# Decayed k tiles used in place as score operands, with every fourth row given to the fourth head pair

## The chip, the cores and the metric

One NeuronCore of one Trainium2 chip runs the whole program. The metric is the device time of one execution in microseconds (us). Kernels are compared by the median of their runs.

## The reference

The inputs are four batches of eight heads, 768 steps, 48 dimensions per head (float32). Three layers follow each other. The change touches the first alone, a linear attention whose state decays by a gate of its own in every dimension of the key:

```
f = sigmoid(f_logit)
for t in range(768):
    state = f[:, :, t, :, None] * state + einsum('bhd,bhe->bhde', k[:, :, t], v[:, :, t])
    y[:, :, t] = einsum('bhd,bhde->bhe', q[:, :, t], state)

x     = y, heads side by side: (4, 768, 384)
theta = x @ w_theta                                   # layer 2
u     = x + w_tok_r @ (x * cos(theta)) + w_tok_i @ (x * sin(theta))
x     = u + relu(u @ w_ch)
h     = relu(x @ w_in)                                # layer 3
out   = (h[:, :, :512] * (w_spatial @ norm(h[:, :, 512:]) + b_spatial)) @ w_out
```

## The kernel before, in words

**Stages.** The program has a prologue (attention of batch 0), then a long mixed stage in which layer 2 of batch b runs among the attention of batch b + 1, and from about 370 us a last stage with layer 3 alone. The change touches nothing of the last stage.

**Chunks and decay.** The 768 steps are cut into 12 chunks of 64. `dense(b, g)` (L494) takes 128 of the 384 rows (head, dimension) of a batch at a time, so that no partition is empty: three dense tiles a batch, twelve in all. It loads f, k and q, makes the running products of the gates inside a chunk (a scan on DVE into `icp`, a logarithm and an exponential on ACT into `cw`) and multiplies k by `icp` and q by `cw`. GpSimd writes the chunks' decay into 12 more columns of the k tile.

**Pairs.** Everything after that goes by pairs of heads, four a batch, 16 in all, numbered u. TensorE works there on quadrants of 64 x 64. A head has only 48 rows, so a pair needs tiles with head 0 in partitions 0 to 47, head 1 in 64 to 111, and zeros between: `KP` (768 + 12 columns) and `QP` (768 columns), two buffers of each, whose zeros are written once. `att_load` (L541) fills them with DMAs from the dense tiles, by runs of at most 48 partitions, split where a head crosses from one dense tile into the next; it loads v in two layouts (`VN`, `VC`) as well.

**Per pair.** `att_s` (L585) makes the scores k^T q of each chunk (tile psc), which DVE masks into `sc`. `att_w` (L557) multiplies the transposed k, tile `KT`, which `att_k` (L530) makes from the dense tile with six transposes (tile pt), by v (tile pw); ACT copies the products out, ACT also spreads the decay over a tile (cu in batch 0, later st or cb), and a DVE scan turns both into the states. For pairs up to `NEAR` the states are read as the scan leaves them, 12 elements apart; for later ones ACT copies them to adjacent elements first (tile st). `att_x` (L603) adds q times state and score times v (tile px), and ACT copies the pair's columns into `X`. Layer 2 of a batch starts with transposes of `X` (tile pt) and can start only when all four pairs are in it. Its large product over the steps has the name acc, the product by w_ch the name hh; tk is a token weight, z a product of x and a sine or cosine, both made on DVE and ACT; ws is a landing tile for weights.

**What sets the order.** Within a stage the program is issued by ticks written by hand (`UNIT`, `KEYS`, `DECAY`, L52 to L58, in `mixes`); a planner (`Plan`) then reorders each engine's list with its own table of durations. Each engine runs its list in that order. All DMAs are issued by one queue, SyncE's, in its own planned order: an issue that has to wait for a tile holds up all behind it. Nearly all instructions are recorded at one helper line, L370 (L371 in the changed kernel), so tiles are told apart by name.

**Buffers.** Dense tiles take turns in `BUFS` buffers (f 1, k 2, q 2); the few in `EARLY` borrow the space of tiles that layer 2 needs later.

Of the kernel before, what the change touches and what calls it, by code (L numbers as in the profile page):

```python
# [21 lines left out]
P = 128  # L22
B, H, S, D = 4, 8, 768, 48
DM = H * D
# [13 lines left out]
PARTS = 4  # L38
BUFS = {"f": 1, "k": 2, "q": 2}

EARLY = {("f", 1): "z10", ("f", 2): "z11", ("k", 2): "z12", ("q", 2): "z13"}

# [7 lines left out]

NEAR = 8
WARM = {("s", 0, 0): 20}  # L52
# [19 lines left out]
class Box:  # L72
    def __init__(self, ap):
        a = ap.bass_ap
        self.t = a.tensor.name
        shape, dims = list(a.tensor.shape), [list(x) for x in a.ap]
        row = math.prod(shape[1:])
        span = lambda d: sum(abs(s) * (n - 1) for s, n in d) + 1
        if dims[0][0] == row and len(dims) > 1:
            self.p = (a.offset // row, a.offset // row + dims[0][1])  # L80
# [310 lines left out]
class Kernel:  # L391
# [75 lines left out]
    def att_open(self, ctx):  # L467
        tc, V, A, G = self.tc, self.V, self.A, self.G
        self.a1 = a1 = self.pool(ctx, "a1", 1, side="left")
        self.a2 = self.pool(ctx, "a2", 2, side="left")  # L470
        self.mask = a1.tile([P, C], F32, name="mask")
        G.memset(self.mask, 1.0)
        for h in range(2):
            m = self.mask[64 * h : 64 * h + 64, :]
            G.affine_select(out=m, in_=m, pattern=[[1, C]], compare_op=ALU.is_ge, fill=0.0, base=0, channel_multiplier=-1)
        self.one = a1.tile([P, NC, C], BF16, name="one")
        G.memset(self.one, 0.0)
        G.memset(self.one[:, :, 0:1], 1.0)
# [4 lines left out]
        self.KP = [a1.tile([P, S + NC], F32, name=f"kp{i}") for i in range(2)]  # L483
        self.QP = [a1.tile([P, S], F32, name=f"qp{i}") for i in range(2)]
        self.SC = [a1.tile([P, S], F32, name=f"sc{i}") for i in range(2)]
        self.KT = a1.tile([P, NT, DM + 64 - D], F32, name="kt")
        for i in range(2):
            G.memset(self.KP[i], 0.0)
            G.memset(self.QP[i], 0.0)
        G.memset(self.KT[:, :, DM:], 0.0)  # L490
        self.dn, self.un = {}, {}


    def dense(self, b, g):  # L494
# [4 lines left out]
        for x in ("f", "k", "q"):  # L499
# [3 lines left out]
            else:  # L503
                t[x] = self.a2.tile([P, w], F32, name=f"{x}{n}", tag=x, bufs=BUFS[x])
            self.Q.dma_start(out=t[x][:, 0:S], in_=self.a[x].rearrange("u r t -> (u r) t")[P * n : P * n + P])
        f, k, q, cx = t["f"][:, 0:S], t["k"][:, 0:S], t["q"][:, 0:S], t["k"][:, S:]
# [23 lines left out]
    def att_k(self, b, g):  # L530
        self.group()
        k = self.dn[3 * b + g]["k"]
        for n in range(0, NT, 3):
            p = self.bank("pt")
            self.warm(p, ("k", b, g, n))
            for i in range(3):
                self.T.transpose(p[:, P * i : P * i + P], k[:, P * (n + i) : P * (n + i) + P], self.ident)
            self.A.activation(self.KT[:, n : n + 3, P * g : P * g + P], p[:, 0:DM].rearrange("p (n d) -> p n d", n=3), AF.Copy)


    def att_load(self, u):  # L541
        b, pr, w = u // NP, u % NP, u % 2
        for x, to in (("k", self.KP[w]), ("q", self.QP[w])):
            for h in range(2):
                r, end = D * (2 * pr + h), D * (2 * pr + h + 1)
                o = 64 * h
                while r < end:
                    m = min(end, r // P * P + P) - r
                    self.Q.dma_start(out=to[o : o + m], in_=self.dn[3 * b + r // P][x][r % P : r % P + m])
                    r, o = r + m, o + m  # L550
        self.Q.dma_start(out=self.VN[w], in_=self.a["vu"][u])
        self.Q.dma_start(out=self.VC[w], in_=self.a["va"][u])
# [4 lines left out]
    def att_w(self, u):  # L557
        self.group()
        V, A, T = self.V, self.A, self.T
        w2 = u % 2  # L560
        KT, VN = self.KT, self.VN[w2]
        if u < NP:
            cu = self.c1.tile([P, 2, D, NC], F32, name=f"cu{u}", tag=f"uT{w2}")
            cb, ub = cu[:, 0], cu[:, 1]
        else:
            far = u >= NEAR
            cb, ub = [self.a2.tile([P, D, NC], F32, name=f"{n}{u}", tag=n, bufs=m) for n, m in (("cb" if far else "st", 2 - far), ("ub", 1))]
        A.activation(cb, self.KP[w2][:, None, S:].to_broadcast([P, D, NC]), AF.Copy)
        w = [self.bank("pw") for _ in range(2)]
        self.warm(w[0], ("w", u))  # L570
        w = [x[:, 0 : 6 * D].rearrange("p (n d) -> p n d", n=NT) for x in w]
        for n in range(NT):
            for s, i in ((0, 0), (1, 1), (1, 0), (0, 1)):
                o, r, h = slice(64 * i, 64 * i + 64), slice(64 * s, 64 * s + 64), 2 * (u % NP) + i
                T.matmul(w[s][o, n], lhsT=KT[r, n, D * h : D * h + 64], rhs=VN[r, i, n], start=True, stop=True)
        for s in range(2):
# [8 lines left out]
    def att_s(self, u, g):  # L585
        self.group()
        V, T = self.V, self.T
        K, Q, sc = self.KP[u % 2], self.QP[u % 2], self.SC[u % 2]
        ps = self.bank("psc", "acc" if u < NP else "att")
# [13 lines left out]
    def att_x(self, u, X):  # L603
        self.group()
        A, T, pr = self.A, self.T, u % NP
        Q, sc, v, st = self.QP[u % 2], self.SC[u % 2], self.VC[u % 2], self.st[u]
        ps = [self.bank("px") for _ in range(2)]
# [521 lines left out]
    def mixes(self, X, sa, sw, se):  # L1129
# [35 lines left out]
        for u in range(NP, B * NP):  # L1165
# [4 lines left out]
            at(t + 2, self.att_s, u, 1)  # L1170
            at(t + XLAG, self.att_x, u, x)
        for g, t in enumerate(DECAY):
            steps(self.dense((g + 4) // 3, (g + 4) % 3), [t + k for k in range(3)])
        for b in range(1, B):
            steps(self.p1_thetas(b, X[b % 2]), [2 * n * (b - 1) + n + t for t in THETA[b - 1]])
# [26 lines left out]
    def run(self):  # L1202
# [26 lines left out]
        for _ in range(FILL):  # L1229
            self.T.matmul(p[:, 0:P], lhsT=self.ident, rhs=self.ident, start=True, stop=True)  # L1230
        self.att_k(0, 0)
        run(merge((dense(0, 1), 9), (self.att_pe(0, X[0]), 6)))
        self.att_k(0, 1)
        run(merge((dense(0, 2), 9), (self.att_pe(1, X[0]), 6)))
        self.att_k(0, 2)
        run(pe(2))
# [58 lines left out]
def layout(inputs):  # L1295
# [5 lines left out]
    def heads(x):  # L1301
        return c(x.transpose(0, 1, 3, 2).reshape(B * NP, 2 * D, S))

    raw = lambda x: x.view(np.uint64) if x.dtype == np.float64 else x
    v = inputs["v"]
# [3 lines left out]
    return {  # L1309
        "q": heads(inputs["q"]),  # L1310
        "k": heads(inputs["k"]),
        "f": heads(inputs["f_logit"]),
        "vt": c(v2.transpose(0, 1, 2, 4, 3).reshape(B * NP, 2, D, S)),
# [24 lines left out]
```

## Time and profile before

| | us |
|---|---|
| runs: 618.46, 618.77, 624.06; median | 618.77 |
| the profiled execution, whole | 619.71 |
| the profiled execution, span of the trace | 617.9 |
| TensorE matmuls busy (5736 instructions) | 589.9 (95%) |
| DVE busy (822) | 457.7 (74%) |
| ACT busy (622) | 332.0 (54%) |
| GpSimd busy (54) | 21.3 (3%) |
| moved by DMA | 146.57 MB, 237 GB/s |

The execution's own time holds 1.8 us around the span. An engine's share over the whole span is a mean over stages with different limits; where TensorE stood idle or was clocked down, and what released it, says more. A busy TensorE is not one at its peak: matmuls overlap, and their ends are modelled.

### The profile page before, as it was taken

Reading aid. Unit: us, or ns where it says so; the run is one execution under the profiler, and the core shown is the slowest. Engines: PE = TensorE matmul, PEld = TensorE weight load, DVE = VectorE, ACT = ScalarE, POOL = GpSimd, SP = SyncE. Lnnn points to the kernel's source line nnn. Section 1 sums busy time; section 2 is a strip of 40 time slices with the busy share of each in tenths; the row PEclk is TensorE's granted clock in tenths of the full one; section 3 lists DMA queues with packets and bytes.
Section 4 is the critical chain, followed back from the end, with each engine's and each line's share of the span. In section 5 each row is a group of like instructions: output and inputs, shape, how many; then the busy total and the mean of one; then the engine's idle time right before and its main releaser. Section 6 shows DMA issues by size and latency. Waiting matters only on the chain.

```text
span 617.9 us, 14127 instructions
## 1 busy us (share of the span) xinstructions
PE 589.9 (95%) x5736; PEld 534.2 (86%) x5736; DVE 457.7 (74%) x822; ACT 332.0 (54%) x622; POOL 21.3 (3%) x54
## 2 busy tenths in 40 slices
PE   8678999999999999989999999999999999999995
PEld 8566556766899899979999988999999999999995
DVE  5776999887799668827998538897659656966681
ACT  4555783558867587736884224533453345345421
POOL 4200010000010000000000000000000000000000
PEclk9967999999999999999999999999999999999998
DMA  7788958989778978888999989598109712950322
GB/s 278 225 259 244 298 191 238 284 289 321 245 215 262 334 267 274 266 271 270 331 307 327 350 284 317 206 339 306 46 15 379 258 39 75 357 192 16 131 101 81
DMA packets 67720, 146.57 MB, mean 237 GB/s; under 512 B 6848, under 2 KB 35264, under 8 KB 67648
## 3 DMA queue, kind: packets, MB, share of 16 engines
q1 hardware_dynamic: 67648, 145.59, 70.4%
q8 instruction: 47, 0.77, 0.5%
q14 instruction: 25, 0.20, 0.1%
HBM read 104.20 MB, written 31.85 MB: 220 GB/s over the span
## 4 chain that ended last, share of the span: by engine, by line
PE 83%; DVE 6%; DMA 5%; issue 2%; ACT 2%; POOL 0%; SPq 0%; DVEq 0%; ACTq 0%
PE acc L370 21%; PE pg L370 14%; PE pu L370 8%; PE pv L370 8%; PE po L370 8%; PE hh L370 6%; PE pth L370 6%; PE px L370 4%; PE psc L370 4%; PE pt L370 3%; DMA kp<-k 2%; PE pw L370 2%; DVE tk L370 2%; DVE icp L370 1%; DMA wpd<-wt 1%
## 5 line engine op out<-in xcount | busy, mean ns | idle before, releaser
L370 PE MATMUL acc<-tk,z 128*128 128x384 f32 x792 | 174.3, 369 | 1.8 <-DVE tk L370 1.2
L370 PEld LDWEIGHTS acc<-tk,z 128*128 128x128 f32 x792 | 137.7, 188 | 18.7 <-DVE tk L370 1.8
L370 PE MATMUL pg<-sp,vn 128*128 128x384 f32 x504 | 88.0, 336 | 0.0
L370 PEld LDWEIGHTS pg<-sp,vn 128*128 128x128 f32 x504 | 87.4, 188 | 0.0
L370 PE MATMUL po<-wo,gt 128*128 128x384 f32 x288 | 52.3, 339 | 0.0
L370 PEld LDWEIGHTS po<-wo,gt 128*128 128x128 f32 x288 | 50.8, 188 | 0.8 <-ACT gt L370 0.5
L370 PE MATMUL pu<-x,wi 128*128 128x384 f32 x288 | 50.7, 334 | 0.0
L370 PEld LDWEIGHTS pu<-x,wi 128*128 128x128 f32 x288 | 50.1, 188 | 0.3
L370 PE MATMUL pv<-wi,x 128*128 128x512 f32 x216 | 50.4, 390 | 0.0
L370 PEld LDWEIGHTS pv<-wi,x 128*128 128x128 f32 x216 | 40.5, 188 | 8.1
L370 PE MATMUL hh<-uT,wc 128*128 128x384 f32 x216 | 42.7, 344 | 1.3 <-DVE xt L370 0.9
L370 PEld LDWEIGHTS hh<-uT,wc 128*128 128x128 f32 x216 | 37.8, 188 | 3.0 <-DVE uT L370 1.3
L370 DVE TENSOR_TENSOR vn<-vr,vn 128x768 fp32r<-128x768 f32 x24 | 22.9, 956 | 19.6 <-ACT vn L370 18.8
L370 ACT ACTIVATE gt<-g 128x384 fp32r<-128x384 f32 x32 | 16.7, 523 | 38.0 <-DVE g L370 38.0
L370 DVE BATCH_NORM_STATS2 st<-vr 128x6 f32<-128x512 f32 x24 | 16.5, 691 | 25.7 <-ACT vr L370 25.6
L370 PE MATMUL psc<-qp,kp 64*64 64x64 f32 x768 | 30.0, 226 | 4.4 <-DMA kp<-k 3.1
L370 PEld LDWEIGHTS psc<-qp,kp 64*64 64x64 f32 x768 | 26.9, 140 | 8.2 <-issue 2.9
L370 PE MATMUL px<-vc,sc 64*64 64x48 f32 x768 | 29.7, 230 | 3.3 <-issue 3.3
L370 ACT ACTIVATE vn<-vr 128x768 fp32r<-128x768 f32 x24 | 20.3, 845 | 21.9 <-PE pg L370 18.8
L370 ACT ACTIVATE ws<-ws 128x768 f32<-128x768 f32 (+2 forms) x28 | 20.6, 740 | 19.5 <-DMA ws<-wo_dram 8.2
L370 PEld LDWEIGHTS px<-vc,sc 64*64 64x64 f32 x768 | 27.3, 150 | 3.8 <-issue 3.6
L370 PE MATMUL pth<-ft,xt 128*128 128x384 f32 x72 | 25.5, 493 | 0.6 <-ACT xt L370 0.6
(128 smaller groups left out, 1002.0 us busy)
## 6 DMA issues: line engine op xcount, KB each, us to landing
sp<-wpd SPq DMA_DIRECT2D x56, 576.0 KB, 6.2
tk<-tkp SPq DMA_DIRECT2D x48, 384.0 KB, 4.9
ws<-tok_dram SPq DMA_DIRECT2D x12, 768.0 KB, 5.7
tkp<-tk SPq DMA_DIRECT2D x24, 384.0 KB, 4.5
f<-f_dram SPq DMA_DIRECT2D x12, 384.0 KB, 5.8
k<-k_dram SPq DMA_DIRECT2D x12, 384.0 KB, 6.0
q<-q_dram SPq DMA_DIRECT2D x12, 384.0 KB, 6.7
vn<-vu_dram SPq DMA_DIRECT2D x16, 288.0 KB, 6.1
```

The source lines that it names most:

```text
L370: r = f(*a, **k)
```

## The change

The rows of q, k and f are put into another order on the way in (`layout`, function `dense`). Each dense tile of 128 rows now holds two heads in two groups of 64 partitions; in each group three rows out of four belong to that head (48 rows), and every fourth (16 rows) belongs to one of the heads 6 and 7. Three dense tiles hold heads 0 to 5 and, in their fourth rows, all 96 rows of heads 6 and 7.

So for three pairs of four the k tile is used where it lies: its foreign rows are made harmless by zeros in q. `att_mask` copies q to `QP` on ACT with a factor per partition, `live`, that is 0 in every fourth row and 1 elsewhere (GpSimd and DVE make it once). The fourth pair alone is gathered by DMA: `att_gap` copies every fourth partition, 32 rows of k and of q from each dense tile (as 16 + 16 from the middle one, where heads 6 and 7 meet), into the one `KP` and the third `QP`. For that pair the columns of `KT` that `att_w` loads as weights stand 4 elements apart.

The k tiles live longer, so they have three buffers and q has one; one more q tile is in `EARLY`; one tick of `DECAY` moves from 51 to 58, and `NEAR` from 8 to 6, so that pairs 6 and 7 also get the copy to adjacent states.

```diff
-BUFS = {"f": 1, "k": 2, "q": 2}
-EARLY = {("f", 1): "z10", ("f", 2): "z11", ("k", 2): "z12", ("q", 2): "z13"}
+BUFS = {"f": 1, "k": 3, "q": 1}
+STEP, GAP = 4, C - D
+EARLY = {("f", 1): "z10", ("f", 2): "z11", ("k", 2): "z12", ("q", 1): "z14", ("q", 2): "z13"}
...
-NEAR = 8
+NEAR = 6
...
-DECAY = [0, 4, 19.5, 36, 40, 45, 51, 73]
+DECAY = [0, 4, 19.5, 36, 40, 45, 58, 73]
...
+        m = a1.tile([P, P // STEP], F32, name="rows")
+        G.memset(m, 1.0)
+        G.affine_select(out=m, in_=m, pattern=[[-STEP, P // STEP]], compare_op=ALU.not_equal, fill=0.0, base=1 - STEP, channel_multiplier=1)
+        V.tensor_reduce(self.live, m, axis=AX.X, op=ALU.min)
...
+    def att_gap(self, b, g):
+        n = 2 * GAP
+        for x, to in (("k", self.KP), ("q", self.QP[2])):
+            gap = self.dn[3 * b + g][x][STEP - 1 : P : STEP]
+            r = n * g
+            while r < n * g + n:
+                i = r // D
+                m = min(n * g + n, D * i + D) - r
+                self.Q.dma_start(out=to[C * i + r % D : C * i + r % D + m], in_=gap[r - n * g : r - n * g + m])
+                r += m
+
+    def att_kq(self, u):
+        b, pr = u // NP, u % NP
+        return (self.dn[3 * b + pr]["k"], self.QP[u % 2]) if pr < 3 else (self.KP, self.QP[2])
+
+    def att_mask(self, u):
+        self.A.activation(self.QP[u % 2], self.dn[3 * (u // NP) + u % NP]["q"], AF.Copy, scale=self.live[:, 0:1])
 
     def att_load(self, u):
-        b, pr, w = u // NP, u % NP, u % 2
-        for x, to in (("k", self.KP[w]), ("q", self.QP[w])):
-            for h in range(2):
-                r, end = D * (2 * pr + h), D * (2 * pr + h + 1)
-                o = 64 * h
-                while r < end:
-                    m = min(end, r // P * P + P) - r
-                    self.Q.dma_start(out=to[o : o + m], in_=self.dn[3 * b + r // P][x][r % P : r % P + m])
-                    r, o = r + m, o + m
+        w = u % 2
         self.Q.dma_start(out=self.VN[w], in_=self.a["vu"][u])
...
-        A.activation(cb, self.KP[w2][:, None, S:].to_broadcast([P, D, NC]), AF.Copy)
+        A.activation(cb, K[:, None, S:].to_broadcast([P, D, NC]), AF.Copy)
...
-                T.matmul(w[s][o, n], lhsT=KT[r, n, D * h : D * h + 64], rhs=VN[r, i, n], start=True, stop=True)
+                if u % NP < 3:
+                    o2, step = DM * n + P * (u % NP) + C * i, 1
+                else:
+                    o2, step = DM * n + STEP * D * i + STEP - 1, STEP
+                k = KT[r, o2 : o2 + (C - 1) * step + 1 : step]
+                T.matmul(w[s][o, n], lhsT=k, rhs=VN[r, i, n], start=True, stop=True)
...
+        def after(n, t):
+            b, g = n // 3, n % 3
+            u = NP * b + g
+            x, y = max(t, done(NP * b - 1)), max(t, done(u - (NP if g == 1 else 2)))
+            at(x, self.att_gap, b, g)
+            at(y, self.att_mask, u)
+            return max(x, y)
```

**Where the order moves.** The first place is ACT's list in the prologue, from the first transposed k on. In it f, q, k are dense tiles (one number each per tile), cu is the state tile of a pair, kp and qp the padded operands. Before:

```order
L370 ACTIVATE kt<-pt 128x3x128 x2
L370 ACTIVATE cw<-icp 128x768
L370 ACTIVATE cw<-cw 128x768
L370 ACTIVATE f_381<-f_381 128x768 x2
L370 ACTIVATE cu_276<-kp_104 128x576
L370 ACTIVATE cu_276<-pw 128x288 x2
L370 ACTIVATE cw<-icp 128x768
L370 ACTIVATE X_129<-px 128x6x48 x2
```

And now:

```order
L371 ACTIVATE kt<-pt 128x3x128 x2
L371 ACTIVATE cu_278<-k_137 128x576
L371 ACTIVATE cu_278<-pw 128x288 x2
L371 ACTIVATE cw<-icp 128x768
L371 ACTIVATE cw<-cw 128x768
L371 ACTIVATE qp_105<-q_139,live 128x768
L371 ACTIVATE f_388<-f_388 128x768 x2
L371 ACTIVATE qp_106<-q_225,live 128x768
L371 ACTIVATE cu_425<-k_223 128x576
```

The masked copies of q for pairs 0 and 1 are new on ACT, and the decay of a pair is read from the k tile itself.

The second place is SyncE's queue at the same time, from the load of the third k tile on. Before:

```order
L370 DMA k_383<-k_dram 128x768
L370 DMA kp_104<-k_134 48x780 x2
L370 DMA qp_106<-q_136 48x768 x2
L370 DMA kp_105<-k_134 32x780
L370 DMA qp_107<-q_136 32x768
L370 DMA vc_103<-va_dram 128x576
L370 DMA q_385<-q_dram 128x768
L370 DMA qp_107<-q_219 48x768
L370 DMA kp_105<-k_217 48x780
L370 DMA qp_107<-q_219 16x768
```

And now:

```order
L371 DMA kp<-k_137 32x780
L371 DMA qp_107<-q_139 32x768
L371 DMA vn_100<-vu_dram 128x576
L371 DMA ws<-wt_dram 128x768 x2
L371 DMA f_755<-fd_dram 128x768
L371 DMA kp<-k_223 16x780 x2
L371 DMA qp_107<-q_225 16x768 x2
L371 DMA k_757<-kd_dram 128x768
L371 DMA q_759<-qd_dram 128x768
L371 DMA vc_102<-va_dram 128x576
```

What is gathered there now is for the fourth pair only, and loads of weights and of the next batch stand earlier among the gathers.

The third place is ACT's list later in the prologue, round the transposes of the third k tile; ws is a weight that has landed. Before:

```order
L370 ACTIVATE f_761<-f_761 128x768
L370 ACTIVATE kt<-pt 128x3x128 x2
L370 ACTIVATE cu_602<-kp_105 128x576
L370 ACTIVATE cu_557<-pw 128x288 x2
L370 ACTIVATE cw<-icp 128x768
L370 ACTIVATE ws<-ws 128x384
```

And now:

```order
L371 ACTIVATE X_132<-px 128x6x48 x2
L371 ACTIVATE ws<-ws 128x384
L371 ACTIVATE cw<-icp 128x768
L371 ACTIVATE ws<-ws 128x384
L371 ACTIVATE kt<-pt 128x3x128 x2
L371 ACTIVATE cw<-cw 128x768
L371 ACTIVATE cu_551<-pw 128x288 x2
```

The copies of the transposes (kt) stood ahead of the weights' first step; now two such steps stand ahead of them.

## Rows read from the trace of the kernel before

**Rows 1.** Stretches of 10 us: each engine's busy time (instructions), TensorE's granted clock, DMA share, GB/s.

```profile
20.00:30.00 10.00, 5.51 (x194) 4.86 (x194) 7.81 (x10) 4.34 (x9) 1.13 (x2) 1.00 0.72 207
30.00:40.00 10.00, 7.00 (x170) 6.43 (x172) 7.40 (x12) 5.56 (x11) 0.88 (x2) 0.56 0.74 221
50.00:60.00 10.00, 9.13 (x120) 6.85 (x113) 5.81 (x12) 6.42 (x15) 0.25 (x2) 0.75 0.86 262
80.00:90.00 10.00, 9.86 (x92) 6.04 (x94) 9.73 (x13) 8.50 (x12) 0.98 (x1) 1.00 0.82 273
160.00:170.00 10.00, 10.00 (x138) 9.13 (x137) 7.40 (x13) 9.83 (x18) 0.00 (x0) 1.00 0.66 226
270.00:280.00 10.00, 8.22 (x202) 7.34 (x198) 4.40 (x8) 3.81 (x7) 0.00 (x0) 1.00 0.87 298
```

**Rows 2.** Chain of waits, 0 to 110 us: start, length, what.

```profile
21.48 3.88 DMA kp<-k
...
30.90 4.28 DMA kp<-k
...
91.96 2.85 PE acc L370 x8
```

**Rows 3.** Timeline of TensorE, 0 to 125 us: start, length, instructions, [idle before <-releaser].

```profile
17.76 1.99 PE L370 MATMUL psc<-qp,kp 64*64 64x64 f32 x48
...
25.61 1.71 PE L370 MATMUL psc<-qp,kp 64*64 64x64 f32 x48 [2.27 <-DMA kp<-k]
...
35.83 1.51 PE L370 MATMUL psc<-qp,kp 64*64 64x64 f32 x22 [0.80 <-DMA kp<-k]
...
53.67 1.48 PE L370 MATMUL pt<-ident,X 128*128 128x128 f32 x6
```

**Rows 4.** Timeline of DVE, 0 to 62 us.

```profile
12.15 0.94 DVE L370 TENSOR_TENSOR q<-q,cw 128x768 f32<-128x768 f32 x1
...
18.65 0.96 DVE L370 TENSOR_TENSOR q<-q,cw 128x768 f32<-128x768 f32 x1
...
26.66 1.26 DVE L370 TENSOR_TENSOR sc<-psc,mask 128x384 f32<-128x384 f32 x2 [1.95 <-PE psc L370]
...
29.81 0.96 DVE L370 TENSOR_TENSOR q<-q,cw 128x768 f32<-128x768 f32 x1
...
44.03 1.35 DVE L370 TENSOR_TENSOR_SCAN cu<-cu 128x576 f32<-128x576 f32 x1
```

**Rows 5.** Instructions by line and shape: count | busy us, mean ns | idle before.

```profile
L370 ACT ACTIVATE f<-f 128x768 f32<-128x768 f32 x24 | 20.2, 843 | 8.7 <-DMA f<-f_dram 8.3
L370 PEld LDWEIGHTS pw<-vn,kt 64*64 64x64 f32 x768 | 13.8, 140 | 7.2 <-issue 5.8 <-ACT kt L370 1.3
L370 ACT ACTIVATE st<-cb 128x528 f32<-128x528 f32 x8 | 9.2, 1155 | 6.7 <-DVE cb L370 6.7
```

**Rows 6.** Stretches of one px each: PE busy, PEld busy, ACT busy, clock, DMA, GB/s.

```profile
20.00:24.00 4.00, 2.06 (x92) 1.80 (x92) 0.00 (x0) 1.00 0.64 167
...
210.00:212.20 2.20, 1.60 (x92) 1.48 (x92) 0.24 (x1) 1.00 0.79 185
```

**Rows 7.** DMA issues (count, KB each, median us to landing), and the spread of kp's.

```profile
kp<-k SPq DMA_DIRECT2D x24, 146.2 KB, 4.0
...
ws<-wc_dram SPq DMA_DIRECT2D x3, 384.0 KB, 5.7
...
kp<-k SPq DMA_DIRECT2D x8, 97.5 KB, 4.8
...
kp<-k SPq DMA_DIRECT2D x8, 48.8 KB, 3.8
...
DMA to landing us min/median/max: 2.5/4.3/7.4
```

**Rows 8.** Chain of waits, 255 to 300 us, and ACT's timeline there.

```profile
263.31 5.10 DMA kp<-k
...
268.51 0.68 ACT L370 ACTIVATE cb<-kp 128x576 f32<-128x576 f32 x1 [2.19 <-DMA kp<-k]
```

More of the change, by code (lines that the diff above doesn't have):

```diff
@@ L78, in __init__ @@
         span = lambda d: sum(abs(s) * (n - 1) for s, n in d) + 1
-        if dims[0][0] == row and len(dims) > 1:
-            self.p = (a.offset // row, a.offset // row + dims[0][1])
+        if dims[0][0] and dims[0][0] % row == 0 and len(dims) > 1:
+            self.p = (a.offset // row, a.offset // row + dims[0][0] // row * (dims[0][1] - 1) + 1)
             self.f = (a.offset % row, a.offset % row + span(dims[1:]))
@@ L482, in att_open @@
         self.VC = [a1.tile([P, NC, D], F32, name=f"vc{i}") for i in range(2)]
-        self.KP = [a1.tile([P, S + NC], F32, name=f"kp{i}") for i in range(2)]
-        self.QP = [a1.tile([P, S], F32, name=f"qp{i}") for i in range(2)]
+        self.KP = a1.tile([P, S + NC], F32, name="kp")
+        self.QP = [a1.tile([P, S], F32, name=f"qp{i}") for i in range(3)]
         self.SC = [a1.tile([P, S], F32, name=f"sc{i}") for i in range(2)]
[L486 to L491, printed above, removed]
+        self.KT = a1.tile([P, NT * DM + C], F32, name="kt")
+        self.live = a1.tile([P, 1], F32, name="live")
+        m = a1.tile([P, P // STEP], F32, name="rows")
+        G.memset(m, 1.0)
+        G.affine_select(out=m, in_=m, pattern=[[-STEP, P // STEP]], compare_op=ALU.not_equal, fill=0.0, base=1 - STEP, channel_multiplier=1)
+        V.tensor_reduce(self.live, m, axis=AX.X, op=ALU.min)
+        G.memset(self.KP, 0.0)
+        G.memset(self.QP[2], 0.0)
+        G.memset(self.KT[:, NT * DM :], 0.0)
+        self.dn = {}
     def dense(self, b, g):
@@ L504, in dense @@
                 t[x] = self.a2.tile([P, w], F32, name=f"{x}{n}", tag=x, bufs=BUFS[x])
-            self.Q.dma_start(out=t[x][:, 0:S], in_=self.a[x].rearrange("u r t -> (u r) t")[P * n : P * n + P])
+            self.Q.dma_start(out=t[x][:, 0:S], in_=self.a[x + "d"][n])
         f, k, q, cx = t["f"][:, 0:S], t["k"][:, 0:S], t["q"][:, 0:S], t["k"][:, S:]
@@ L560, in att_w @@
         w2 = u % 2
-        KT, VN = self.KT, self.VN[w2]
+        KT, VN, K = self.KT, self.VN[w2], self.att_kq(u)[0]
         if u < NP:
@@ L587, in att_s @@
         V, T = self.V, self.T
-        K, Q, sc = self.KP[u % 2], self.QP[u % 2], self.SC[u % 2]
+        (K, Q), sc = self.att_kq(u), self.SC[u % 2]
         ps = self.bank("psc", "acc" if u < NP else "att")
@@ L605, in att_x @@
         A, T, pr = self.A, self.T, u % NP
-        Q, sc, v, st = self.QP[u % 2], self.SC[u % 2], self.VC[u % 2], self.st[u]
+        Q, sc, v, st = self.att_kq(u)[1], self.SC[u % 2], self.VC[u % 2], self.st[u]
         ps = [self.bank("px") for _ in range(2)]
@@ L1171, in mixes, with done @@
             at(t + XLAG, self.att_x, u, x)
+        def done(u):
+            return UNIT[u - NP] + XLAG + 0.1 if u >= NP else 0
+        def after(n, t):
[5 more added lines that the diff above has]
+            return max(x, y)
+        after(3, -1)
         for g, t in enumerate(DECAY):
             steps(self.dense((g + 4) // 3, (g + 4) % 3), [t + k for k in range(3)])
+            assert after(g + 4, t + 2.5) < [*DECAY, 99][g + 1]
         for b in range(1, B):
@@ L1231, in run @@
         self.att_k(0, 0)
+        self.att_gap(0, 0)
+        self.att_mask(0)
         run(merge((dense(0, 1), 9), (self.att_pe(0, X[0]), 6)))
+        self.att_gap(0, 1)
+        self.att_mask(1)
         self.att_k(0, 1)
         run(merge((dense(0, 2), 9), (self.att_pe(1, X[0]), 6)))
+        self.att_gap(0, 2)
+        self.att_mask(2)
         self.att_k(0, 2)
@@ L1302, in heads, with dense @@
         return c(x.transpose(0, 1, 3, 2).reshape(B * NP, 2 * D, S))
+    def dense(x):
+        m, i, r = np.meshgrid(np.arange(3), np.arange(2), np.arange(C), indexing="ij")
+        n = (2 * m + i) * GAP + r // STEP
+        gap = r % STEP == STEP - 1
+        head = np.where(gap, 6 + n // D, 2 * m + i)
+        dim = np.where(gap, n % D, r // STEP * (STEP - 1) + r % STEP)
+        return c(x.reshape(B, DM, S)[:, (D * head + dim).reshape(-1)].reshape(3 * B, P, S))
+    q, k, f = (heads(inputs[x]) for x in ("q", "k", "f_logit"))
     raw = lambda x: x.view(np.uint64) if x.dtype == np.float64 else x
@@ L1309, in layout @@
     return {
-        "q": heads(inputs["q"]),
-        "k": heads(inputs["k"]),
-        "f": heads(inputs["f_logit"]),
+        "q": q,
+        "k": k,
+        "f": f,
+        "qd": dense(q),
+        "kd": dense(k),
+        "fd": dense(f),
         "vt": c(v2.transpose(0, 1, 2, 4, 3).reshape(B * NP, 2, D, S)),
```

5 lines of the change are left out of this document (3 added, 2 removed).

## The prediction

> **What bounds the kernel now.** I read the stretches of 10 us first. From about 60 us to the end TensorE is busy almost without a break, so little can be won there except what shortens its own list: 9.86 of 10 us in the stretch from 80, 10.00 in that from 160 [rows 1]. Two places are different. In the prologue TensorE works only 5.51 and 7.00 us of the stretches from 20 and 30 us. [...] The second place is the stretch from 270 us, with 8.22 us.
>
> The chain of waits says what those places wait for. In the prologue it goes twice through the copy of decayed k rows into the padded tile, 3.88 and 4.28 us [rows 2]. TensorE's timeline agrees: the scores of pair 1 start at 25.61 and those of pair 2 at 35.83, each released by that DMA [rows 3]. Near 263 us the chain takes the same copy once more, 5.10 us [rows 8]. The change takes most of these copies away, so I cost the chain step by step.
>
> **Prologue: the hop of pair 1.** DVE has q of dense tile 1 ready at 18.65 + 0.96 = 19.61 [rows 4]; its scores start at 25.61 [rows 3], 6.0 us later, by way of two queued copies. Now one ACT instruction stands there instead. No mask was ever run, but an ACT copy of the same 128 x 768 takes 0.84 us [rows 5]. In the new order DVE does the scan of pair 0 ahead of this q (one scan of that shape is 1.35 us [rows 4]), and some small work in between goes behind it, so I put q at about 20.2 and the scores at 21.1, 4.5 us earlier. Pair 0 gains nothing: a run of warm-up products stands ahead of its scores in both orders, and its q, ready at 12.15 + 0.94 = 13.1 [rows 4], leaves time enough for a mask before 17.76 [rows 3].
>
> **Prologue: the hop of pair 2.** DVE stood 1.95 us until pair 1's scores came [rows 4]. Without that wait the product for q of tile 2, which ended at 29.81 + 0.96 = 30.77, ends at about 28.8. Its scores then start at 28.8 + 0.1 + 0.84, about 29.8, not 35.83: 6.0 us earlier. Pair 3 still needs its gather, of the last 32 rows of k and of q, after the same product. Such a copy takes 2.5 to 7.4 us to land, 4.3 in the middle [rows 7], so its scores start between 32 and 35: 1 to 4 us earlier. It no longer stands in front of pair 2, whose work fills that time.
>
> **Prologue: what is left of it.** From the scores at 35.83 to the first transposes of X at 53.67 [rows 3] lies a chain through the last scan at 44.03 [rows 4] and the products px. If only DVE's own wait goes, it moves by 2.0 us; if the whole stretch follows pair 2, by 6.0. I take **-5.0**, nearer the upper end, because two weight loads go ahead of the gathers in the queue and DVE's conversions move up with them. I don't take the end itself, because a new wait is there: ACT's copies of the third transposed tile now stand behind the first step on a wc weight, whose load takes 5.7 us to land [rows 7] and is issued only when an older landing tile has been read. The prologue's lead should last, since TensorE runs nearly closed from the product at 91.96 on [rows 1, 2].
>
> **The weights of pair 3.** For one pair in four the 64 columns of KT that are loaded as weights stand 4 elements (16 bytes) apart. A pair has 48 such loads (24 products in two passes), 192 over four batches. No load of the trace is strided; an adjacent one takes 140 ns [rows 5]. The nearest row is the px of pair 0, which reads 44 state operands with elements 12 apart: TensorE is 2.06 us at it, against 1.60 for a pair with copied states, at the same clock [rows 6]. That is 0.46 / 44 = 10 ns an operand. I take 192 x 0.010 = **+1.9**. The lower end is 0. For the upper one I take the strided ACT copy of the states, 1155 ns for 528 elements, 2.2 each, against 843 for 768, 1.1 each [rows 5]: a stride that doubles the price. A load of 280 ns with nothing hidden is 192 x 0.140 = +26.9. I stay at the px, since it is TensorE's own.
>
> [...]
>
> **NEAR.** Pairs 6 and 7 get adjacent states: 2 x 0.46 = **-0.9** on TensorE, for two ACT copies of 1.16 us [rows 5, 6]. The pairs' states are then a copy later, which nothing in the steady stage waits for as long as TensorE has products of layer 2 to do.
>
> **The stall at 263 us.** There ACT waits 2.19 us for the decay columns of a gathered k [rows 8] and TensorE lacks 1.78 us of the stretch from 270 [rows 1]. Three pairs of four no longer need that copy. I take **-1.0**, between 0 (the next wait, that for the states, is as late) and -1.8.
>
> **At nothing.** Twelve masks are 12 x 0.84 = 10.1 us more on ACT; three are costed above. ACT works 3.8 to 8.5 us of 10 in most stretches [rows 1], so the other nine fit. Where the cover fails, as in the stretch from 160 with 9.83, each costs up to 0.84, for two of them +1.7. DMA issues fall from 80 to 32. By the sizes of rows 7 a batch's k copies go from (6 x 146.2 + 2 x 97.5 + 2 x 48.8) = 1170 KB to (2 x 97.5 + 2 x 48.8) = 293 KB, and q's nearly alike: 1.8 MB a batch, some 7 us of DMA at the 250 GB/s of these stretches. I book no gain, since no other transfer ends the chain in the prologue; it is the cover under which the loads moved ahead can land. The gathers add waits in SyncE's queue, for GpSimd's columns; behind them stand loads of the next batch, wanted tens of us later. The k tiles are held longer, and a later tick and a third buffer keep loads out of their way. The new tiles and the memsets at the start lie beside the first loads.
>
> **Sum.** -5.0 + 1.9 - 0.9 - 1.0 = -5.0 against the profiled execution's 619.71, so 614.7. That execution is 0.94 above the median of the runs, 618.77, so I forecast **613.8** (611 to 617), with a chance of 0.45. A measurement of this kernel can't tell less than 1%, 6.2 us, from no change: 612.6 and 625.0 are the borders.
>
> **Rival 1: the clock goes with the gaps.** With TensorE's idle time shorter, the low clock may not come. Its 7.00 us busy at 0.56 would be 3.9 at full clock, its 9.13 at 0.75 would be 6.8 [rows 1]: up to 5.4 us more, and 613.8 - 5.4 = 608.4. For it: the low clock comes right behind the longest idle. Against it: pair 3's gather and the wait for the weight leave a gap, and small products on quadrants stay as they are. Chance 0.25.
>
> **Rival 2: DVE takes the lead back.** In the stretch from 80 us DVE is busy 9.73 of 10, and the product at 91.96 waits for its work on a token weight [rows 1, 2]. If the weights of layer 2, not X, set that time, an earlier X only waits longer: the -5.0 and the -1.0 go, +1.9 and -0.9 stay, 619.8. Against it: DVE idles 4.2 us of the stretch from 50 [rows 1], room that the weights could use. Chance 0.17.
>
> **Rival 3: slower, by the strided weights.** [...] Without this part the sum is -6.9; over 192 loads it is eaten up at 36 ns a load, and the kernel is over 1% slower from (6.9 + 6.2) / 192 = 68 ns on, half an adjacent load. At the upper end the time is 618.8 - 6.9 + 26.9 = 638.8. For it: the only strided operand seen was a moving one. Against it: 10 ns there, with four quadrants at work. Chance 0.13.
>
> That the change doesn't do what it says is no rival: the masks and the gathers of 32 and 16 rows stand in the order.
>
> **Range and chances.** From 606.5, which leaves out only the far end of rival 1, to 621.5, which holds rival 2 and leaves out rival 3. Faster by over 1%: most of rival 1 and three tenths of the forecast's own range, 0.24 + 0.14 = 0.38. Slower: rival 3 and a little for mishaps of the new order, 0.15. Within: 0.47.
>
> **What would show it.** In the new trace: the scores of pair 1 at about 21 us and of pair 2 at about 30; no copy of k ahead of either in the chain; the first transposes of X at 48 to 50; DVE without a wait for pair 1's scores. The clock from 30 to 60 us decides rival 1. If X is 5 us earlier and the first product behind 90 us isn't, it is rival 2. The load time of pw for pairs 3, 7, 11 and 15, against 140 ns, and TensorE's time at such a pw decide rival 3. The forecast is wrong if the time from X to the end of the mixed stage grows by more than 2 us, whatever the prologue does.

## The result, and the profile after

The changed kernel takes 611.78 us (median of 4 runs, 610.61 to 612.93), the kernel before 618.89 in the same comparison: a ratio of 0.9864 with an interval of 0.9817 to 0.9912, 7.1 us less. The forecast was 613.8 in a range of 606.5 to 621.5. The profiled execution took 612.93 us, its span is 611.2, 6.7 below the span before. The page of the changed kernel, its span, its engines and its DMA:

```profile
span 611.2 us, 14027 instructions
PE 588.2 (96%) x5736; PEld 535.8 (88%) x5736; DVE 457.5 (75%) x823; ACT 347.3 (57%) x638; POOL 22.9 (4%) x54
DMA packets 64648, 139.43 MB, mean 228 GB/s; under 512 B 6080, under 2 KB 34496, under 8 KB 64576
```

Of those 6.7 us, TensorE's idle time is 5.0 (611.2 - 588.2 = 23.0, before 617.9 - 589.9 = 28.0) and its busy time 1.7. The stretches of 10 us say where. Columns as in [rows 1]; the changed kernel:

```profile
20.00:30.00 10.00, 6.62 (x212) 5.93 (x214) 9.17 (x16) 8.55 (x16) 2.01 (x3) 0.85 0.71 247
30.00:40.00 10.00, 8.54 (x232) 8.08 (x228) 8.20 (x14) 4.72 (x10) 0.98 (x1) 0.64 0.64 197
40.00:50.00 10.00, 7.47 (x233) 6.97 (x232) 9.79 (x16) 5.74 (x14) 0.30 (x2) 0.70 0.67 189
50.00:60.00 10.00, 8.37 (x123) 6.46 (x123) 5.23 (x9) 7.02 (x15) 0.00 (x0) 0.96 0.84 281
100.00:110.00 10.00, 8.06 (x198) 5.87 (x194) 8.61 (x14) 6.77 (x13) 0.00 (x0) 1.00 0.79 254
200.00:210.00 10.00, 10.00 (x142) 9.66 (x141) 6.62 (x10) 5.08 (x9) 1.07 (x3) 1.00 0.90 327
270.00:280.00 10.00, 10.00 (x231) 8.82 (x233) 5.08 (x8) 4.61 (x10) 0.00 (x0) 1.00 0.42 144
360.00:370.00 10.00, 9.43 (x45) 7.64 (x44) 9.89 (x20) 5.72 (x10) 0.00 (x0) 1.00 0.83 290
370.00:380.00 10.00, 10.00 (x47) 8.44 (x47) 6.86 (x21) 4.34 (x11) 0.00 (x0) 1.00 1.00 320
```

And four stretches of the kernel before that the forecast did not use:

```profile
40.00:50.00 10.00, 7.07 (x282) 6.71 (x280) 8.87 (x15) 4.55 (x10) 0.20 (x1) 0.84 0.92 305
200.00:210.00 10.00, 8.81 (x215) 8.28 (x215) 8.14 (x11) 5.70 (x11) 0.25 (x2) 1.00 0.96 330
360.00:370.00 10.00, 9.02 (x46) 7.58 (x46) 4.57 (x9) 3.26 (x6) 0.00 (x0) 1.00 0.81 306
370.00:380.00 10.00, 9.09 (x44) 7.59 (x43) 8.74 (x18) 4.74 (x9) 0.00 (x0) 1.00 0.87 321
```

Ten less the first number of a row is TensorE's idle time there. Added up over all such rows it is a ledger of the gain:

| TensorE idle, us | before | after | difference |
|---|---|---|---|
| 0 to 60 (prologue) | 13.47 | 11.86 | -1.6 |
| 60 to 120 (start of the mixed stage) | 3.05 | 3.78 | +0.7 |
| 200 to 210 | 1.19 | 0 | -1.2 |
| 270 to 280 | 1.78 | 0 | -1.8 |
| 360 to 380 (end of the mixed stage) | 1.89 | 0.57 | -1.3 |
| 0 to 380, all | 21.38 | 16.21 | -5.2 |

So the prologue, on which the forecast put 5 us, gives a third of that, and three later places give the rest. The ledger compares one execution with one. That the last of these places belongs to the change is not shown: from 360 to 380 us TensorE idles 1.20 us in the run below with the bytes put back and 1.19 with NEAR 8, which are as free of the copies, and 0.52 in the kernel before with the tuned numbers.

The ledger does not say what TensorE waited for. Over the whole program it waits 3.1 us for copies of k in the kernel before, at two places of [rows 3], and 2.6 us for masked copies of q in the changed one. A larger item is another. Six waits of the kernel before, 7.3 us together, have no releaser that the profile shows; the profile calls them "issue". They stand in the middle of a run of products, whose operands are in use already. Three of them, from its chain of waits:

```profile
44.35 2.56 issue
...
205.44 1.19 issue
...
275.44 1.61 issue
```

The other three are 0.87 us at 50.86, 0.70 at 103.52 and 0.41 at 117.14. Each of the six ends 1.2 to 1.6 us after the end of one of the 47 transfers, of 16 KB each, that the profile lists as instructions:

```profile
q8 instruction: 47, 0.77, 0.5%
```

And if TensorE's records in the trace (weight loads, products and its sequencer's own) are counted from 0, each wait ends at a record whose number divided by 256 leaves 193. The same two things hold of all 27 waits of this kind over 0.1 us in the 14 traces of this document. From these two regularities the author infers that TensorE waits there for the next block of its own instructions, and they are called waits for instructions below; no run takes such a wait away by itself to prove it. The changed kernel has one such wait, in the products by w_ch:

```profile
111.00 1.23 PE L371 MATMUL hh<-uT,wc 128*128 128x384 f32 x6 [1.13 <-issue]
```

So the waits for instructions fall by 6.2 us, from 7.3 to 1.1, and all other idle time of TensorE rises by 1.2, from 20.7 to 21.9. Of the ledger, the 1.2 us from 200 and 1.6 of the 1.8 from 270 us are waits for instructions; before 60 us 3.4 us of them went, while other waits there grew by 1.8.

TensorE's timeline of the changed kernel answers to [rows 3]:

```profile
17.30 1.61 PE L371 MATMUL psc<-qp,k 64*64 64x64 f32 x48
20.66 1.44 PE L371 MATMUL psc<-qp,k 64*64 64x64 f32 x42 [1.75 <-ACT qp L371]
29.05 1.55 PE L371 MATMUL psc<-qp,k 64*64 64x64 f32 x24 [0.90 <-ACT qp L371]
34.34 1.48 PE L371 MATMUL psc<-qp,kp 64*64 64x64 f32 x22
51.11 0.82 PE L371 MATMUL pt<-ident,X 128*128 128x128 f32 x6
75.57 4.68 PE L371 MATMUL acc<-tk,z 128*128 128x384 f32 x14
```

The scores of pairs 1 and 2 are now released by the mask on ACT and start 4.95 and 6.78 us earlier than in [rows 3]. Pair 3 keeps its gather and starts at 34.3. The transposes of X are only 2.6 us earlier. By the last row 1.4 us of this are left: the group of acc at 75.57 begins with the 17th of these products, and the 17th starts at 76.98 in the kernel before.

DVE's timeline, two rows that answer to [rows 4] and the first token weight, then ACT's row of that weight's landing tile, and the masks as a group (columns as in [rows 5]):

```profile
23.56 1.01 DVE L371 TENSOR_TENSOR sc<-psc,mask 128x384 f32<-128x384 f32 x2
27.07 0.96 DVE L371 TENSOR_TENSOR q<-q,cw 128x768 f32<-128x768 f32 x1
55.34 0.56 DVE L371 TENSOR_SCALAR tk<-ws 128x768 uint32<-128x768 uint32 x1 [4.63 <-ACT ws L371]
...
54.40 0.90 ACT L371 ACTIVATE ws<-ws 128x768 f32<-128x768 f32 x1 [1.84 <-DMA ws<-tok_dram]
...
L371 ACT ACTIVATE qp<-q,live 128x768 f32<-128x768 f32 x12 | 11.2, 936 | 9.3 <-DVE q L371 9.3
```

DVE no longer waits for pair 1's scores, and q of tile 2 is done at 28.03, not 30.77. But at 55.34 DVE has waited 4.63 us for ACT, which waited for the first token weight to land.

The chain of waits of the changed kernel, whose only copy of k before 110 us is now one of 1.24 us at 97.91:

```profile
41.71 4.57 DMA ws<-wc_dram
47.86 6.46 DMA ws<-tok_dram
...
97.91 1.24 DMA kp<-k
```

Where [rows 2] had copies of k, loads of weights stand: of wc, and of the first token weight.

At the end of the mixed stage the chain of the kernel before went through two transfers, of a token weight written out and read back, and of a weight of layer 3:

```profile
356.02 6.20 DMA tk<-tkp
...
362.28 8.19 DMA wpd<-wt
```

In the changed kernel neither is in the chain there. In the kernel before TensorE itself waits 0.57 us for the first, at 362.70, and 0.91 for work of DVE that comes behind the second, at 370.73. The forecast did not look there; as said above, it is not shown that the change is what removed this.

### The profile page after: what moved, and what is told of

It is laid out like the page before. It is cut to its first block, busy times and chain, and to the rows that moved or that the text cites. A ratio compares the mean times of both kernels' runs of the same rounds, so it can differ in the third digit from the quotient of the medians.

```text
span 611.2 us, 14027 instructions
## 1 busy us (share of the span) xinstructions
PE 588.2 (96%) x5736; PEld 535.8 (88%) x5736; DVE 457.5 (75%) x823; ACT 347.3 (57%) x638; POOL 22.9 (4%) x54
## 4 chain that ended last, share of the span: by engine, by line
PE 84%; DVE 6%; DMA 5%; ACT 2%; issue 1%; SPq 0%; POOL 0%; ACTq 0%; DVEq 0%; POOLq 0%
PE acc L371 26%; PE pg L371 12%; PE pu L371 8%; PE pv L371 8%; PE po L371 7%; PE pth L371 6%; PE hh L371 6%; PE psc L371 3%; PE px L371 3%; PE pt L371 2%; PE pw L371 2%; DMA xs<-x2d 1%; DMA ws<-tok_dram 1%; DMA ws<-wt_dram 1%; DMA ws<-wc_dram 1%
## 5 line engine op out<-in xcount | busy, mean ns | idle before, releaser
L371 DVE TENSOR_TENSOR vn<-vr,vn 128x768 fp32r<-128x768 f32 x24 | 22.9, 956 | 18.9 <-ACT vn L371 18.1
L371 ACT ACTIVATE sn<-sn 128x384 f32<-128x384 f32 x48 | 24.2, 515 | 3.9 <-DVE sn L371 3.9
L371 ACT ACTIVATE oo<-po 128x384 f32<-128x384 f32 x24 | 11.8, 492 | 25.5 <-PE po L371 19.8
```

What stands on the lines that cost most here:

```text
L371: r = f(*a, **k)
```

## The experiments

Each is one edit of the changed kernel, unless it says that the kernel before was edited. Ratios are against runs of the kernel before taken beside them, whose median was 620.4 to 621.2 us; the changed kernel's own ratio, to compare with, is 0.9864.

**Adjacent weights for the fourth pair.** The diff:

```diff
-                    o2, step = DM * n + STEP * D * i + STEP - 1, STEP
+                    o2, step = DM * n + STEP * D * i, 1
```

> The changed kernel, but pairs 3, 7, 11 and 15 load adjacent columns of KT as weights (other columns than theirs, so that their states are of other rows); order and everything else stay as they are. In the changed kernel's trace such a pw takes 1.66 us, the other pairs' 0.92. If the stride is what costs, the four pw take 0.92 each, and the time falls by up to 4 x 0.74 = 3.0 us, to about 609; the three in the mixed stage, where TensorE is closed, should give at least 1.5. If TensorE waits there for something else anyway, the pw get shorter and the time stays at 611.8.

609.47 us (608.18 to 612.59), ratio 0.9836 [0.9793, 0.9879]. The interval overlaps the changed kernel's, so the runs alone do not tell a difference; the trace does. TensorE is busy 584.9 us, 3.3 less. A pw of the fourth pair takes 1.66 us with the stride and 0.92 without, 0.74 a pair and 3.0 for four: the stride costs that, in place of the 1.9 forecast.

**Other steps.** Pair 3 keeps step 4, pairs 7, 11 and 15 get steps 2, 3 and 6.

```diff
-                    o2, step = DM * n + STEP * D * i + STEP - 1, STEP
+                    step = {3: 4, 7: 2, 11: 3, 15: 6}[u]
+                    o2 = DM * n
```

> The changed kernel with pair 3 as it is (columns 4 apart) and pairs 7, 11 and 15 loading columns 2, 3 and 6 apart (others than theirs): one look at the length of each one's pw. [...] If any step costs alike, all three take 1.66; if it grows with the step, pair 15 takes over 2.

One run, 611.03 us. What matters is TensorE's timeline at the four pw, here in the order of steps 4, 2, 3, 6:

```profile
39.32 1.65 PE L371 MATMUL pw<-vn,kt 64*64 64x48 f32 x46 [0.34 <-ACT cu L371]
...
113.22 0.94 PE L371 MATMUL pw<-vn,kt 64*64 64x48 f32 x48
...
190.97 1.26 PE L371 MATMUL pw<-vn,kt 64*64 64x48 f32 x48
...
269.98 1.58 PE L371 MATMUL pw<-vn,kt 64*64 64x48 f32 x48
```

And two of the changed kernel, an adjacent pair and the fourth one after it:

```profile
105.20 0.92 PE L371 MATMUL pw<-vn,kt 64*64 64x48 f32 x48
...
116.75 1.66 PE L371 MATMUL pw<-vn,kt 64*64 64x48 f32 x48
```

Step 2 costs nothing (0.94 against 0.92), step 3 about half of the penalty (1.26), step 4 all of it, and step 6 no more (1.58). So the steps do not all cost alike, and from 4 to 6 the price does not grow. Why, these runs do not show.

The weight loads' own records show the penalty as well, but not its size. The loads of the changed kernel at 105.2 and at 116.75 us (count, busy us, mean ns of one):

```profile
L371 PEld LDWEIGHTS pw<-vn,kt 64*64 64x64 f32 x48 | 0.8, 134 | 0.5 <-ACT X L371 0.5
...
L371 PEld LDWEIGHTS pw<-vn,kt 64*64 64x64 f32 x48 | 1.5, 211 | 0.3 <-issue 0.3
```

A load grows by 77 ns, but the 48 loads together by 0.7 us, 15 ns each, since their records overlap: the 48 add up to 6.4 us in 0.8 us of busy time at 134 ns, and to 10.1 us in 1.5 at 211.

**The copies put back, everywhere.** Masked q and k with its decay columns are copied onto themselves for all twelve in-place pairs, as 48 rows a head, so that scores and states wait for DMAs of the old size again. The results are the same.

```diff
+            for h in range(2):
+                t = self.QP[u % 2][C * h : C * h + D]
+                self.Q.dma_start(out=t, in_=t)
...
+    def hop(self, u):
+        if u % NP < 3:
+            for h in range(2):
+                t = self.att_kq(u)[0][C * h : C * h + D]
+                self.Q.dma_start(out=t, in_=t)
```

> The changed kernel with the copies put back for all twelve pairs that are used in place, of k with its decay columns and of the masked q, 48 rows a head onto themselves: operands, masks, weights and buffers are the changed kernel's, but scores and the spread of the decay wait for a copy as before. If the waits for the copies are where the gain is, the time rises by 6 to 10 (the 7 that were won and up to 3 for the strided weights, which stay), to 618 to 622. If the gain came from the new buffers, ticks and order, it stays under 615.

626.51 us (623.07 to 629.2), ratio 1.0105 [1.0063, 1.0147]: 15 us above the changed kernel, and slower than the kernel before. TensorE's waits from 10 to 60 us (us in total, times, longest), its largest row:

```profile
PE psc L371 <- DMA k<-k: 7.7, 5, 2.8
```

And its stretches:

```profile
20.00:30.00 10.00, 8.56 (x186) 7.62 (x189) 7.70 (x9) 6.07 (x12) 2.00 (x3) 0.52 0.84 244
30.00:40.00 10.00, 6.05 (x148) 5.56 (x143) 7.34 (x14) 5.76 (x10) 1.18 (x1) 0.50 0.94 285
40.00:50.00 10.00, 7.57 (x165) 6.71 (x162) 8.54 (x13) 4.80 (x11) 1.02 (x2) 0.50 0.79 255
```

Its span is 621.3 and its TensorE busy 594.1, so its idle time is 27.2 us, against 23.0 in the changed kernel: copies that scores wait for cost this order 4.2 us of idle time. That is nearly the 28.0 of the kernel before, but it is not the same idle time. TensorE waits 8.9 us for copies here (7.7 for k, 1.2 for q), and 3.1 in the kernel before; for instructions 2.3 us here, and 7.3 there. Even pair 0 waits for its copies, its scores start at 19.98 us against 17.76 in the kernel before, and X starts at 57.85 against 53.67. So the run shows what such copies would cost the changed kernel, and not that the old ones cost the kernel before as much.

TensorE is also busy 5.9 us longer. In the three stretches from 20 to 50 us the granted clock is 0.52, 0.50 and 0.50. As an estimate from the rows, busy time times (1 - granted clock), summed over the four stretches from 20 to 60 us, is 11.3 us here, 6.6 in the changed kernel and 6.5 before. That is 4.7 of the 5.9 us. Against the kernel before, the idle time is 0.8 us less and the busy time 4.2 more, so by this estimate it is the clock that puts this kernel above it.

**Only q's copies, in the prologue, and only in the later batches.** The first lines of that diff, under `if u < NP`, and under `if u >= NP`.

> The changed kernel with the hop put back in the prologue: after the mask of pairs 0, 1 and 2 two DMAs of 48 rows copy the masked q onto itself, so that the scores wait for a copy again as they did before. By my forecast's step (the prologue's lead is worth 5) the time rises by 4 to 5, to 616. By the rival read from the new trace (the first products of layer 2 wait for the loads of its weights through two landing tiles, so an earlier X is lost again by 76 us) X comes 2 to 4 us later and the time stays within 1.5 us of 611.8.

> The changed kernel with the same hop put back for the nine pairs of batches 1 to 3 that are used in place, the prologue as changed. If the gain came from the waits near 205 and 263 us, which were copies of k and q, the time rises by 2 to 4, to 614 to 616, with TensorE idle there again. If those waits went because the planner put the pairs elsewhere, the time stays within 1.5 of 611.8.

In the prologue: 615.6 us (611.72 to 617.99), 0.9922 [0.9883, 0.9961], 3.6 us of the gain lost for three pairs, though the interval still overlaps the changed kernel's a little. In the other batches: 612.73 us (610.73 to 621.04), 0.9888 [0.9836, 0.994], 1.5 us for nine pairs, which the intervals do not tell from nothing. In the first trace X starts at 53.21, 2.1 us later than in the changed kernel; TensorE waits 1.4 us for copies of q and 2.1 for instructions. In the second, of the slowest execution of the six, it waits once for a copy of q, 2.11 us before 278.30, and once for instructions, 2.05 us before 207.59.

**The bytes put back.** The k and q rows of the in-place pairs are copied to DRAM, where nobody reads them.

```diff
+        t = self.dn[3 * (u // NP) + u % NP]
+        for x in ("k", "q"):
+            n = S + NC if x == "k" else S
+            for h in range(2):
+                z = self.dr.tile([D, n], F32, name=f"copy{x}{u}{h}")
+                self.Q.dma_start(out=z, in_=t[x][C * h : C * h + D])
```

> The changed kernel with the traffic put back and nobody waiting for it: after each mask the 48 rows of k and q of both heads are copied to DRAM that nothing reads, 48 issues of 144 to 146 KB, about the 7 MB and the 48 issues that the change took away. If the relief of the DMA engines and of the queue is what gives the gain, the time rises by 4 to 7, to 616 to 619. If the waits for the copies were the cost, it stays within 2 of 611.8.

611.37 us (610.08 to 612.96), 0.985 [0.9808, 0.9891], at the 146.57 MB of the kernel before. So neither the 7 MB nor the 48 issues by themselves are the gain. TensorE waits for instructions 0.8 us here, so the bytes alone do not bring those waits back either.

**The tuned numbers.** NEAR back to 8 in the changed kernel, and NEAR 6 with the later tick alone in the kernel before:

```diff
-NEAR = 6
+NEAR = 8
```

```diff
-NEAR = 8
+NEAR = 6
...
-DECAY = [0, 4, 19.5, 36, 40, 45, 51, 73]
+DECAY = [0, 4, 19.5, 36, 40, 45, 58, 73]
```

> The changed kernel with NEAR back at 8: pairs 6 and 7 read their states 12 elements apart again. The forecast's step gives 2 x 0.46 = 0.9 more, 612.7. If the planner's new order from this one number matters more than the pairs' own 0.9, the time moves by 2 or more either way.

> The kernel before with the two numbers that the change also sets, NEAR 6 and the DECAY tick 58, and nothing else. If the new order that follows from such numbers is part of the gain, the time falls by 2 or more; if the gain is in the copies alone, it stays within 1.5 of the kernel before.

NEAR 8: 613.75 us (612.61 to 614.68), 0.9893 [0.9854, 0.9931], 2 us more with overlapping intervals. The kernel before with the new numbers: 619.63 us (616.75 to 623.65), 0.9995 [0.9965, 1.0026]. By themselves they bring nothing, and TensorE waits 7.7 us for instructions there, as in the kernel before.

**No loads of w_ch.** The first theory of what swallows the prologue's lead was the landing of these weights, with ACT and DVE behind it.

```diff
-            self.weight(self.wc[0][:, j], self.wc[1][:, j], self.a["wc"][P * j : P * j + P, :], self.c2)
+            for i in range(2):
+                self.G.memset(self.wc[i][:, j].bitcast(F32), 0.0)
```

> The changed kernel without loading w_ch: its tiles are filled with zeros by GpSimd, so three loads and conversions leave the chain of weights that goes through two landing tiles in the prologue (the product with w_ch is of zeros). If that chain of weights, not X, sets when layer 2 starts, the first token weight lands some 5 us earlier, X keeps its lead, and the time falls by 3 to 6, to 606 to 609. If X sets it, the time stays within 1.5 of 611.8.

613.81 us (613.26 to 616.23), 0.9891 [0.9854, 0.9929]: not faster, and the theory fell. Its chain of waits:

```profile
41.73 6.94 DMA ws<-tok_dram
52.31 7.75 DMA ws<-tok_dram
99.96 6.95 DMA ws<-tok_dram
```

The token weights have taken the place of wc: take one weight away, and the next is late.

**No conversion of the first token weights.** In batch 0 plain rows of k stand in for them, in the changed kernel and in the kernel before (there with that kernel's own names).

```diff
-            self.single(f, self.a["tok"][th, c], self.c2)
+            self.Q.dma_start(out=f, in_=self.a["kd"][NT * th + c])
```

> The changed kernel with batch 0's twelve token weights taken as they are from plain float32 rows of k (384 KB each by one DMA, no landing tile, no conversion on ACT and DVE; the weights are wrong). Read beside the same edit of the kernel before. If the token weights' way through two landing tiles is what swallows the prologue's lead, the changed kernel without them starts its steady products at least 2.5 us earlier than the kernel before without them, keeps that to 110 us, and the pair differs by 8 or more. If something else swallows it, the leads at 75 us are alike (under 1 us) here too and the pair differs by about 7.

> The same edit of the kernel before. Both theories: some 30 us of DVE and 5 MB of loads leave the stretch from 60 to 130 us, so the time falls by 3 to 10 from the kernel before; how far it stays above the changed kernel with the edit tells the theories apart (8 or more, or about 7).

The changed kernel: 611.33 us (610.18 to 612.18), 0.9862 [0.9822, 0.9902], no change. The kernel before: 614.42 us (610.8 to 616.48), 0.9908 [0.9873, 0.9942], 6.6 below its own time. Neither theory's number came: without this work the two kernels lie 3.1 us apart. The waits of TensorE from 60 to 120 us, first in the changed kernel, then in the one before:

```profile
PE acc L371 <- DVE xt L371: 1.8, 1, 1.8
PE hh L371 <- issue: 1.1, 1, 1.1
```

```profile
PE acc L370 <- DVE tk L370: 1.2, 1, 1.2
```

None of these three is left once the token weights are gone, though the second is a wait for instructions and not for a token weight. TensorE's idle time from 60 to 120 us falls from 3.8 to 0.7 us in the changed kernel and from 3.1 to 1.0 in the one before; 1.1 us of either fall are waits for instructions. So work on the token weights does limit this stretch, in both. But each kernel has 2.0 to 2.5 us more idle time before 60 us (13.8 against 11.9, 16.0 against 13.5), of which the waits for instructions make 1.5 and 1.0. What the kernel before gains beyond that lies mainly in the stretch from 270 us, where 0.15 us of idle time is left of 1.78, though its copies are still there: the wait for instructions at 275.44 does not come. Why, these runs do not show.

**Sixteen gap rows last.** The foreign rows lie behind the 48 in each 64 rather than among them, and ACT puts the heads side by side in KT by two copies, so that all weights are adjacent. The results are the same.

```diff
-            gap = self.dn[3 * b + g][x][STEP - 1 : P : STEP]
...
+            for h in range(2):
+                r = GAP * (2 * g + h)
+                o = C * (r // D) + r % D
+                self.Q.dma_start(out=to[o : o + GAP], in_=self.dn[3 * b + g][x][C * h + D : C * h + C])
...
+                o2 = DM * n + D * (2 * (u % NP) + i)
+                k = KT[r, o2 : o2 + C]
```

> A version that should beat both: in each group of 64 rows the 16 rows of heads 6 and 7 are the last 16, not every fourth, and ACT's copies of the transposes put the heads side by side in KT, in two instructions for one, so that all pairs load adjacent columns as weights. The four strided pw get 0.74 shorter each, 3.0 in all; 24 more ACT instructions cost ACT about 24 x 0.2 = 5 us beside other work, some of it ahead of pw in the prologue (2 x 0.3 a tile). The gathers take 48 DMA issues, not 32. Expected 609.5, between 608 and 613; if ACT's copies come late for pw, over 612.

610.68 us (608.69 to 614.73), 0.9837 [0.9795, 0.988]. Its median is below both kernels, but 1.1 us below the changed one with such intervals is no difference that was shown. ACT's copies of the transposes are busy 14.4 us there, 24 of 411 ns and 24 of 264, against 10.4 us in the changed kernel, 24 of 488: 4.0 us more for 24 more instructions.

## Why the prediction was right, and where not

**The time and the sign** were right, 2.0 us from the forecast, but not by the sum that gave it. The two waits for copies of k did go, 3.1 us, with 2.6 us of waits for masks in their place. The idle time that the change saved lies in the waits for instructions, 7.3 us before and 1.1 now, which the text did not have. Two of them, at 44.35 and 50.86, lie in the chain to X, and the text took that stretch for a way through the last scan and px alone. So it is in good part luck that the numbers agree.

That these waits go with the change is more than one execution: they are 6.6 to 7.7 us in the kernel before and its two variants, 0 to 1.7 in the changed kernel and the seven variants of it in which no scores wait for a copy put back, and 2.0 to 2.3 in the three in which they do. What in the change removes them is not shown. The tuned numbers alone do not, and bytes or copies put back return a part at most; the third buffer for k and the new order of the engines' lists were not run by themselves.

**Prologue, -5.0: mis-sized.** Its first steps held: the scores at 20.66 and 29.05, forecast 21.1 and 29.8, and DVE without its wait. Pair 3 started within its 32 to 35. The step that failed is that the stretch up to X follows pair 2 nearly whole: X starts at 51.11, 2.6 us earlier and not 5. Even that is not the copies' alone, for the 17.8 us from the scores at 35.83 to X at 53.67 held 3.4 us of waits for instructions, and the changed kernel has none before X. TensorE's idle time up to 50 us fell from 12.60 to 10.23. Nor did the lead last, as the text had said: at 76 us it is 1.4. The first token weight landed late, DVE waited 4.63 us for it, and from 60 to 120 us TensorE idles 0.7 us more than before (3.78 against 3.05; the variants with adjacent weights and with other steps have 1.51 and 2.57 there). This is Rival 2's mechanism in part, the token weights and not X; but its price was wrong, since it let the gain at 263 us go too.

**Strided weights, +1.9: measured +3.0**, 15 ns a load in place of 10. The px of pair 0 was the right neighbour and a lower bound. Rival 3 fell, though the record of a load grew by 77 ns, more than the 68 that it named as the border: that border took each load for itself, and their records overlap (48 of 211 ns in 1.5 us).

**NEAR, -0.9:** the group px with state and q is busy 18.9 us, before 19.7, so -0.8. The runs with NEAR 8 point the same way.

**The stall at 263 us, -1.0:** the 1.78 us from 270 went, but they were not this stall. 1.61 of them are a wait for instructions inside one pw, with 41 products ahead of it and 7 behind, and 0.2 a wait for copied states. So ACT's wait for the decay columns hardly reached TensorE, and the term came true by luck.

**At nothing:** the masks took 936 ns, not 843, and TensorE waits for none of the later ones. But 1.2 us from 200 and 1.3 from 360 us came that the forecast had not. The first was a wait for instructions, in the middle of a pair's scores before 206.62; the second is not shown to belong to the change.

**Rival 1** fell. The stretches of the low clock, which is 0.50 in both traces, moved earlier, from 31.1 and 48.2 us to 27.0 and 44.0, but lasted as long, 10.2 and 6.8 us (means now 0.85, 0.64, 0.70 and 0.96 from 20, 30, 40 and 50 us), and the estimate of what they cost stayed, 6.6 us against 6.5.

**What would have made it wrong**, a longer way from X to the end of the mixed stage, did not come. From X to the first product pv it is 366.62 - 51.11 = 315.5 us, before 319.7.

**Open** stays why the waits for instructions come in the kernel before. All six waits stand among short products on quadrants, 173 of them in the 4.3 us ahead of the first; the busy share of the DMA engines is 1.01 and 1.03 during those at 44.35 and 205.44, but 0.77 during that at 275.44. Of TensorE's busy time, -1.7, the stride and NEAR explain +2.2; of the remaining -3.9 the transposes of k and X and the warm-up products at the start make some 2.0 by their groups, and the rest was not traced. Executions of one kernel spread by 2 us and more, of the kernel before by 9, so no difference under half a per cent was told here.

## What to carry to other kernels

Sum TensorE's idle time by stretches before and after to see which places paid, and then ask of each wait what released it: here the copies that were taken away had held TensorE 3.1 us, and most of the gain lay in waits of another kind. A wait without a releaser in the middle of a run of products is worth comparing with the transfers of instructions. When a prologue is shortened, the next load in the queue can become its end, as that of the first token weight did here (6.46 us in the chain), so ask which weight must have landed for the stage behind it before booking the whole lead. And price a longer weight load by the time between products on all quadrants (15 ns more a load here), not by its own record (77 ns more).

## What the runs showed of the hardware

- Float32 weight loads of 64 x 64 with four quadrants at work: 48 products take 0.92 us at a step of 1 element, 0.94 at 2, 1.26 at 3, 1.66 at 4 and 1.58 at 6. The record of one load goes from 134 to 211 ns at step 4, the time of the 48 together by 15 ns a load.
- TensorE stood idle without a releaser in the middle of a run of products: 27 such waits of 0.1 to 3.8 us in 14 traces, each at the same place of a group of 256 of its records and each ending 1.2 to 1.6 us after a 16 KB transfer of instructions. That they are waits for its own instructions is inferred from this.
- With all copies put back, the granted clock was 0.50 to 0.52 for 30 us of the prologue, which by the estimate cost more than the added idle time there (4.7 against 2.2 us). Idle time alone did not set it: the kernel before without token weights idles 16.0 us before 60, more than the 14.0 of that run, and the estimate there is 6.3 and not 11.3.
- An ACT copy of 128 x 768 with a factor per partition took 936 ns, one in place on f 843.
